# A fused attention and mixture-of-experts kernel: its attention steps issued in another order

## The chip, the cores and the metric

The kernel runs on one NeuronCore of a Trainium2 chip. Time is device time of one execution in microseconds (us); lower is better. The core has four compute engines, each with its own instruction queue that is worked off in order: TensorE (PE in the profile; its weight loads are PEld), VectorE (DVE), ScalarE (ACT) and GpSimd (POOL). SyncE (SP) issues nearly all DMA transfers, in order too. Engines wait for each other through semaphores. TensorE writes its results to PSUM, in banks of 512 f32 per partition; everything else lies in SBUF, 128 partitions wide.

## The reference

Attention over 4 batches, 8 heads, 768 positions of 64 numbers, with a window of 96 positions back, 8 global keys and a bias by distance; then a soft mixture of 8 experts with 4 slots each:

```python
scores = scale * np.matmul(q, k.transpose(0, 1, 3, 2)) + bias   # bias = -slope * distance
scores = np.where(is_global | is_local, scores, -1e9)
a = np.exp(scores - np.max(scores, axis=-1, keepdims=True))
a = a / (np.sum(a, axis=-1, keepdims=True) + 1e-09)
attn = np.matmul(a, v)                       # x: 3072 tokens x 512
...
logits = x @ phi                             # 3072 x 32 slots
d = softmax(logits, over tokens);  slot_input = d.T @ x
h = np.maximum(slot_input[e] @ w1[e], 0);  slot_out[e] = h @ w2[e]   # for each expert e
return softmax(logits, over slots) @ slot_out
```

## The kernel before

Attention is worked off in 16 pairs u of two heads (i = 0, 1), four pairs to a batch. Positions are cut into 7 tiles of 120, and each key tile meets 216 queries; a pair's scores are computed in three steps k = 0, 1, 2 (two, two and three key tiles; the last has 12 matmuls, the others 8). The work is written as steps, small functions that issue a few instructions on one engine. The steps and their engines:

- SyncE: load_qk(u) (832 KB into one of two buffers raw0, raw1), load_v(u), and the experts' weights: 32 pieces of 1 MB. `piece(k)` loads one of the first ten into a buffer of its own; `extra` loads into holes of attention's buffers; `free(i)` loads into a part of an attention buffer once attention is done with it (raw, tb, ph, v16, vt, tt, xta, xtt, xn). A load waits in the queue until what it overwrites has been read, and all loads behind it wait as well.
- TensorE: scores(u,k) (line 522) into one of two PSUM tiles sc0, sc1 by turns; max_t(u), max_b(u) (a transpose and a broadcast of the pair's maximum, lines 538 and 544); values(u,i) (39 matmuls with 39 weight loads, line 579) into x; tr(u,k) (transposes of the result, line 616, four tiles and three); logits(u) for two pairs at a time (line 646); once per batch by_token (line 702) and dispatch (28 matmuls, line 725). `warm` issues matmuls whose result nobody reads.
- VectorE: biased(u,k) (scores plus bias table, with a running maximum, line 531); max_r(u) (line 541); v_lo(u) (line 500, what of V the f16 copy loses); ev_sums, ev_recs, ev_mul(u,i) (division by the sum, lines 592 to 604); the tables; logits_all, strip_max, strip_sum, dispatch_sum once per batch; and tr_copy_dve and w_lo_dve, copies of steps that are else on other engines.
- ScalarE: max_c(u) (line 548), exponential(u,i) (line 552), w_hi(u,i) (the cast to f16, line 555), v_hi_act(u) (line 496), tr_copy (line 621), by_token_copy, lnat_copy, strip_exp.
- GpSimd: w_lo(u,i,part) (what the cast lost, in three parts, line 562), and v_hi for some pairs (line 493).

A pair therefore goes scores, biased, max_t, max_r, max_b, max_c, exponential, w_hi, w_lo, values, ev_mul, tr, tr_copy, logits. The buffers for the cast weights are single for each i (ph0, ph1), so w_hi(u+1,i) waits for values(u,i). The maxima, the transposes, the logits and the dispatch share two PSUM banks (m) by turns. Several pairs are under way at once.

What stands where in each engine's queue is set by one list, ORDER (line 51): 632 entries such as `('scores', 3, 1)`, issued from front to back:

```python
for name, u, *args in ORDER:
    steps[name](u, *args)
```

Each engine gets its own steps in the order of the list; how entries for different engines stand to each other also sets which write counts as earlier, and so some waits. The order of the `free` entries also sets which attention buffer takes which weight piece (`held`). Behind the list come the last batch's softmax and dispatch (last_dispatch), then hidden for two groups of four experts, project, and combine with the output.

Of the kernel before, what the change touches and what calls it, by code (L numbers as in the profile page):

```python
# [1121 lines left out]
```

## Time and profile before

| | us |
|---|---|
| median of 3 runs | 211.16 (210.53 to 211.30) |
| the profiled execution, first to last instruction (span) | 208.9 |
| TensorE busy | 180.1 (86% of the span) |
| VectorE busy | 145.4 (70%) |
| ScalarE busy | 129.5 (62%) |
| GpSimd busy | 105.2 (50%) |
| mean granted TensorE clock | 0.968 of full speed |
| read from HBM, written | 54.59 MB, 6.29 MB |

The profile is of one more execution; for it only the span is known, and it stands 2.3 below the median of the timed runs, which also count what lies around the first and the last instruction. Lines of the profile name an engine, a line of the code, an operation, and out<-in by tile names. In a timeline a row is start, duration, engine, line, operation, tiles, shapes and count; in brackets stands the idle time of the engine just before it and what ended it. Attention's last step, the second half of logits(15), ends near 147 us; the experts' layers fill the rest.

### The profile page before, as it was taken

What the parts mean: (1) busy time and instruction counts of PE and PEld (TensorE: products, weight loads), DVE (VectorE), ACT (ScalarE), POOL (GpSimd) and SP (SyncE); (2) the same over time, 40 slices, a digit from 0 to 9 for tenths busy, and PEclk for the clock granted to TensorE, in tenths of its full rate; (3) what the DMA queues carried; (4) which work ended last, traced back from release to release, by engine and by line L of the source; (5) the groups of instructions that cost most, each with busy time, mean ns of one, the idle gap of its engine ahead of it and who ended that gap; (6) DMA issues with size and microseconds to landing.
All of it is one profiled execution on the core that took longest, in us unless ns stands there. A gap on an engine that the chain in (4) does not pass through costs nothing. (4 is left out here: it accounts for less than half of the span.)

```text
span 208.9 us, 6433 instructions
## 1 busy us (share of the span) xinstructions
PE 180.1 (86%) x2645; PEld 131.2 (63%) x2645; DVE 145.4 (70%) x358; ACT 129.5 (62%) x177; POOL 105.2 (50%) x130
## 2 busy tenths in 40 slices
...
GB/s 109 424 351 393 362 402 397 318 404 416 413 410 370 283 125 135 212 42 254 166 89 244 81 340 354 349 419 367 375 109 326 407 403 387 286 162 344 283 339 108
DMA packets 20631, 61.40 MB, mean 294 GB/s; under 512 B 1904, under 2 KB 9328, under 8 KB 18928
## 3 DMA queue, kind: packets, MB, share of 16 engines
...
q8 instruction: 23, 0.38, 0.7%
...
q10 hardware_dynamic: 144, 0.00, 0.0%
HBM read 54.59 MB, written 6.29 MB: 291 GB/s over the span
## 5 line engine op out<-in xcount | busy, mean ns | idle before, releaser
L562 POOL TENSOR_TENSOR ph<-tb,ph 128x432 f16<-128x432 f32 x92 | 96.6, 1081 | 33.1 <-ACT ph L555 27.7
L522 PE MATMUL sc<-raw 64*128 64x216 f32 (+2 forms) x448 | 48.3, 343 | 3.9 <-DVE mx L531 3.4
L555 ACT CAST ph<-tb 128x1296 f16<-128x1296 f32 x32 | 40.7, 1271 | 9.5 <-PE x L579 8.4
L579 PE MATMUL x<-v,ph 128*128 128x65 f16 (+1 forms) x1248 | 43.6, 194 | 2.7 <-DVE xmax L604 2.2
L579 PEld LDWEIGHTS <-ph 128*128 128x128 f16 x1248 | 40.9, 98 | 7.0 <-issue 5.6
L552 ACT ACTIVATE tb<-tb,nb 128x1296 f32<-128x1296 f32 x32 | 44.0, 1378 | 0.4
L522 PEld LDWEIGHTS sc<-raw 64*128 64x128 f32 x448 | 36.6, 186 | 10.0 <-DVE mx L531 5.0
L604 DVE CUSTOM_DVE_ANT_1 xn<-x,rc 120x448 f32<-120x448 f32 x32 | 19.2, 622 | 4.0 <-PE x L579 3.4
L500 DVE SCALAR_TENSOR_TENSOR v<-vt,v 128x896 f16<-128x896 f32 x16 | 19.8, 1238 | 1.1 <-ACT v L496 1.0
L531 DVE CUSTOM_DVE_ANT_1 tb<-sc,tt,mx 128x864 f32<-128x864 f32 x16 | 17.8, 1113 | 0.9 <-DVE mx L531 0.2
L616 PE MATMUL m<-ident,xn 120*128 120x120 f32 x105 | 14.8, 273 | 2.4 <-DVE xmax L604 1.0
L496 ACT ACTIVATE v<-vt 128x896 f16<-128x896 f32 x12 | 11.3, 944 | 7.4 <-DMA vt<-in_v_dram 7.4
L616 PEld LDWEIGHTS m<-ident,xn 120*128 120x128 f32 x105 | 10.7, 141 | 5.0 <-issue 1.7
L136 PE MATMUL x<-wp,tb 128*32 128x256 f32 x112 | 10.9, 381 | 1.1 <-DVE flag L862 1.1
L106 PE MATMUL hp<-wp,sl 128*32 128x512 f32 x80 | 10.5, 593 | 0.0
L531 DVE CUSTOM_DVE_ANT_1 tb<-sc,xta,mx 128x864 f32<-128x864 f32 x8 | 8.9, 1116 | 1.3 <-PE sc L522 0.8
L531 DVE CUSTOM_DVE_ANT_1 tb<-sc,tt 128x864 f32<-128x864 f32 x8 | 8.5, 1056 | 1.3 <-PE sc L522 0.7
L531 DVE CUSTOM_DVE_ANT_1 tb<-sc,xtt,mx 128x864 f32<-128x864 f32 x8 | 8.9, 1112 | 0.2
L199 ACT COPY ph<-cp 128x512 f32<-128x512 f32 x4 | 2.1, 590 | 10.9 <-PE cp L196 10.9
L136 PEld LDWEIGHTS x<-wp,tb 128*32 128x32 f32 x112 | 5.5, 110 | 3.8 <-DVE flag L862 1.2
L181 DVE TENSOR_SCALAR ohs<-x,sgn 128x256 fp32r<-128x256 f32 x2 | 1.0, 484 | 9.4 <-PE ft L861 4.9
L548 ACT COPY nb<-m 128x1 f32<-128x1 f32 x16 | 2.5, 157 | 7.7 <-PE m L544 7.6
...
## 6 DMA issues: line engine op xcount, KB each, us to landing
raw<-in_qk_dram SPq DMA_DIRECT2D x15, 832.0 KB, 6.3
...
```

The source lines that it names most:

```text
L106: nc.tensor.matmul(out=hp[n][32 * s:32 * s + 32, :], lhsT=slv(a, c, s), rhs=w1(e, c // 2)[:, (c % 2) * DF + 512 * n:(c % 2) * DF + 512 * n ...
L136: nc.tensor.matmul(out=o[32 * s:32 * s + 32, 0:w], lhsT=ht[:, c, 32 * s:32 * s + 32], rhs=w2(4 * a + s, half)[:, c0 + c * w:c0 + c * w + w ...
L496: nc.scalar.activation(out=vhi[u % 2][:, :, :, 0:D], in_=vraw[u % 2], func=AF.Copy, scale=V_SC)
L500: nc.vector.scalar_tensor_tensor(out=vlo[k].rearrange("p j i d -> p (j i) d"), in0=vraw[k].rearrange("p j i d -> p (j i) d"), scalar=V_SC, ...
L522: nc.tensor.matmul(out=z[:, i, at:at + n], lhsT=r_[r, KCOL[j]:KCOL[j] + KR], rhs=r_[r, KW + KB * j:KW + KB * j + n], start=True, stop=True)
L531: nc.vector.tensor_tensor_reduce(out=tb(u)[:, :, BW * k:BW * k + BW], in0=sc[(3 * u + k) % 2][:, :, 0:BW], in1=table.unit(u % NP, k), scal ...
L552: nc.scalar.activation(out=t, in_=t, func=AF.Exp, bias=nbs[u], scale=T_SC)
L555: nc.scalar.copy(out=blocks(phi_[i])[:, :, 0:QW], in_=tb(u)[:, i].rearrange("p (s c) -> p s c", c=QW))
L562: (engine or nc.gpsimd).tensor_tensor(out=blocks(plo_[i])[:, c, 0:QW], in0=tb(u)[:, i].rearrange("p (s c) -> p s c", c=QW)[:, c], in1=bloc ...
L579: nc.tensor.matmul(out=x[:, (D + 1) * t:(D + 1) * t + d], lhsT=w[:, c:c + P], rhs=vv[:, j, i, 0:d], start=(z == 0), stop=(z == len(ops) - ...
L604: nc.vector.tensor_tensor_reduce(out=xnb[(u // 2) % 3][:, :, c:c + D], in0=xv[:, i, :, 0:D], in1=rcs.pop((u, i)).unsqueeze(2).to_broadcast ...
L616: nc.tensor.transpose(out=m[:, at:at + KB], in_=xnb[(u // 2) % 3][:, t, P * (p % 2):P * (p % 2) + P], identity=ident[0:KB, 0:KB])
```

## The change

Only ORDER changes: the same 632 entries in another order. It has no effect on what is computed. The first entries of the list, before and after:

```diff
-ORDER = [('load_qk0', 0), ('load_qk', 0), ('load_v', 0), ('load_qk', 1), ('keys', 0), ('load_v', 1), ('scores', 0, 0), ...
+ORDER = [('keys', 0), ('load_qk0', 0), ('warm', 0, 7), ('table_even', 0), ('table_odd', 0), ('scores', 0, 0), ...
```

Over the whole list, scores steps that follow each other directly on TensorE go from 8 to 13, tr steps from 11 to 4, values steps from 4 to 1. On SyncE the first three pairs' loads of Q and K go ahead of the first piece, phi is loaded later, pieces 3 to 8 are spread over the time up to pair 13, and piece 9 stands at the very end, behind all `free` entries. The three places that matter most:

At the start, on TensorE, from scores(1,0) (raw_94 is pair 1's buffer) to the warm matmuls (L511). Before:

```order
L522 MATMUL sc_173<-raw_94 128x216 x4
L538 MATMUL m<-ident,mx 1x128
L522 MATMUL sc_172<-raw_94 128x216 x4
L544 MATMUL m<-mm_161,bsel 128x1
L511 LDWEIGHTS const-bfloat16-1.0
```

and after:

```order
L522 MATMUL sc_173<-raw_94 128x216 x4
L538 MATMUL m<-ident,mx 1x128
L544 MATMUL m<-mm_161,bsel 128x1
L522 MATMUL sc_172<-raw_94 128x216 x4
L522 MATMUL sc_173<-raw_94 128x216 x2
L522 MATMUL sc_173<-raw_94 128x168 x2
L522 MATMUL sc_173<-raw_94 128x48 x2
L511 LDWEIGHTS const-bfloat16-1.0
```

The maximum of pair 0 (L544) moved ahead of scores(1,1), and scores(1,2) ahead of the ten warm matmuls. A little later max_b(1) moves ahead of values(0,0) in the same way, and on VectorE v_lo(0) and v_lo(1) move from ahead of pair 1's biased steps to between them.

At the third dispatch, on TensorE, behind values(13,1): tr(12,1) and tr(12,0) (L616), the dispatch (L725), max_t(15) (L538) and max_b(15) (L544). Before:

```order
L616 MATMUL m_2255<-ident_78,xn01_106 128x120 x3
L725 MATMUL m_2265<-xn01_106,dn_2259 32x256 x4
L725 MATMUL m_2265<-xn2_105,dn_2259 32x256 x4
L725 MATMUL m_2265<-xn01_106,dn_2259 32x256 x3
L725 MATMUL m_2265<-xn2_105,dn_2259 32x256 x3
L538 MATMUL m_2290<-ident_78,mx_2115 1x128
L616 MATMUL m_2295<-ident_78,xn01_106 128x120 x4
L544 MATMUL m_2290<-mm1_162,bsel_160 128x1
```

and after, where max_t(15) stands ahead of values(13,1) already:

```order
L616 MATMUL m_2260<-ident_78,xn01_106 128x120 x3
L544 MATMUL m_2211<-mm1_162,bsel_160 128x1
L725 MATMUL m_2276<-xn01_106,dn_2208 32x256 x4
L725 MATMUL m_2276<-xn2_105,dn_2208 32x256 x4
L725 MATMUL m_2276<-xn01_106,dn_2208 32x256 x3
L725 MATMUL m_2276<-xn2_105,dn_2208 32x256 x3
```

The last pair's maximum moved ahead of the dispatch; tr(12,0) moved behind values(14,1), where it stands with tr(13,1) and tr(13,0) ahead of values(15,0).

In the same place on ScalarE, from the second exponential of pair 14 (nb_2161, nb_2151) to the second cast of pair 15 (ph1_99). Before:

```order
L552 ACTIVATE tb2_97<-tb2_97,nb_2161 128x1296
L555 CAST ph1_99<-tb2_97 128x6x216
L496 ACTIVATE v16_100<-vt_101 128x14x64
L548 COPY nb_2343<-m_2290 128x1
L621 COPY xta_103<-m_2295 128x480
L552 ACTIVATE tb0_95<-tb0_95,nb_2343 128x1296
L555 CAST ph0_98<-tb0_95 128x6x216
L621 COPY xtt_104<-m_2349 128x480
L552 ACTIVATE tb0_95<-tb0_95,nb_2343 128x1296
L555 CAST ph1_99<-tb0_95 128x6x216
```

and after:

```order
L552 ACTIVATE tb2_97<-tb2_97,nb_2151 128x1296
L621 COPY xta_103<-m_2260 128x288
L548 COPY nb_2271<-m_2211 128x1
L555 CAST ph1_99<-tb2_97 128x6x216
L552 ACTIVATE tb0_95<-tb0_95,nb_2271 128x1296
L496 ACTIVATE v16_100<-vt_101 128x14x64
L555 CAST ph0_98<-tb0_95 128x6x216
L552 ACTIVATE tb0_95<-tb0_95,nb_2271 128x1296
L621 COPY xta_103<-m_2377 128x480
L555 CAST ph1_99<-tb0_95 128x6x216
```

max_c(15) (L548) moved ahead of the second cast of pair 14, and pair 15's first exponential ahead of v_hi_act(15).

2 lines of the change are left out of this document (1 added, 1 removed).

## Prediction

> **What bounds the kernel now.** I read the page for the span and the costliest groups, then busy time by stage, then TensorE's waits, then the timelines of the stages that wait. On the page, the span, two groups (their mean duration stands behind the comma) and one line of the DMA issues (the last number is the median time to landing):
>
> ```profile
> span 208.9 us, 6433 instructions
> ...
> L562 POOL TENSOR_TENSOR ph<-tb,ph 128x432 f16<-128x432 f32 x92 | 96.6, 1081 | 33.1 <-ACT ph L555 27.7
> ...
> L552 ACT ACTIVATE tb<-tb,nb 128x1296 f32<-128x1296 f32 x32 | 44.0, 1378 | 0.4
> ...
> raw<-in_qk_dram SPq DMA_DIRECT2D x15, 832.0 KB, 6.3
> ```
>
> Busy time by stage: start, the even middle, the close of attention, and all that follows it. Behind the length stand PE, PEld, DVE, ACT and POOL with their counts, then TensorE's clock, the DMA share and GB/s:
>
> ```profile
> 0.00:26.00 26.00, 20.70 (x167) 12.14 (x168) 19.87 (x48) 11.76 (x13) 11.43 (x41) 1.00 0.87 328
> 26.00:117.00 91.00, 88.48 (x1524) 73.70 (x1524) 77.94 (x187) 80.22 (x102) 76.83 (x75) 1.00 0.72 269
> 117.00:147.00 30.00, 24.74 (x426) 18.68 (x423) 18.83 (x48) 20.79 (x32) 16.94 (x15) 0.94 0.95 338
> 147.00:209.00 62.00, 46.15 (x536) 26.69 (x536) 28.80 (x76) 16.77 (x33) 0.00 (x0) 0.92 0.81 293
> ```
>
> TensorE idles 2.5 us in the 91 of the middle: there it is the bound. It idles 5.3 us in the 26 of the start and 5.3 in the 30 of the close, where the clock is also below 1. The last 62 us hold none of the reordered steps. Its waits by releaser (total, times, longest):
>
> ```profile
> PE sc L522 <- DVE mx L531: 3.4, 5, 1.3
> PE x L579 <- DVE xmax L604: 2.2, 2, 1.8
> ...
> PE m L702 <- ACT ex L686: 0.9, 1, 0.9
> ```
>
> So a new order can win in the start and in the close, where waits are; in the middle it can win only by making TensorE's own work shorter.
>
> **Nothing is added or removed.** The two tables hold the same 632 steps, so the terms are waits, changes between kinds of work on TensorE, and what the clock does.
>
> **Start.** Rows of the timelines (start, duration, and in brackets the idle time before, with its releaser):
>
> ```profile
> 13.05 1.09 DVE L500 SCALAR_TENSOR_TENSOR v<-vt,v 128x896 f16<-128x896 f32 x1
> ...
> 16.40 1.06 DVE L531 CUSTOM_DVE_ANT_1 tb<-sc,tt 128x864 f32<-128x864 f32 x1
> ```
>
> ```profile
> 22.45 0.38 PE L544 MATMUL m<-mm,bsel 2*128 2x1 f32 x2
> ...
> 25.04 1.00 PE L522 MATMUL sc<-raw 64*128 64x216 f32 x8 [1.21 <-DVE mx L531]
> 25.98 1.36 PE L579 MATMUL x<-v,ph 128*128 128x65 f16 x39
> ```
>
> ```profile
> 22.87 0.16 ACT L548 COPY nb<-m 128x1 f32<-128x1 f32 x1 [2.60 <-PE m L544]
> ```
>
> ```profile
> 25.87 5.84 POOL L562 TENSOR_TENSOR ph<-tb,ph 128x432 f16<-128x432 f32 x6 [1.90 <-ACT ph L555]
> ```
>
> ```profile
> 18.63 0.33 SPq L389 DMA_DIRECT2D raw<-in_qk_dram  x1
> ```
>
> These are v_lo(0); the first bias of pair 1; max_b(1), scores(3,0), values(0,1); max_c(1); the first low parts of pair 1; and load_qk(3). Before, VectorE runs v_lo(0), max_r(0), two tables and v_lo(1) ahead of pair 1's first bias at 16.40. Now only one table and max_r(0) stand ahead, the bias comes at about 14.0, and both v_lo are spread between the biases. The maximum of pair 1 is no longer behind values(0,0) on TensorE (a values step is about 1.3 us): max_c(1) goes from 22.87 to about 21.1, and its exponentials with it, so GpSimd's 1.90 us idle ahead of pair 1 nearly closes. scores(3,0) is put down to VectorE, whose bias had left that bank at 22.4; what came at 25 was load_qk(3), issued 18.63 plus the median 6.3. Now scores(1,2) stands ahead of the ten warm matmuls, load_qk(3) leaves some 2.4 us sooner, and fewer weight pieces share the DMA. Against it: v_hi_act(1), 0.94, now stands between pair 0's first exponential and its cast, where the exponential is only 0.5 us sooner, so pair 0's low parts end 0.3 later than before's 23.97 (25.87 less 1.90). values(0,1) then comes at 24.4 instead of 25.98. I take **-1.5**; the ends are -1.9 (all of GpSimd's idle time) and +0.4 (only the v_hi_act remains, if the load lands no earlier). The warm matmuls put ahead of scores(0,0) cost nothing: the first bias waits for the tables until 9.5, and two score steps take 2 us from 6.9.
>
> **Middle.** TensorE's rows; a step's cost is the distance to the next start:
>
> ```profile
> 45.10 0.91 PE L616 MATMUL m<-ident,xn 120*128 120x120 f32 x7
> 45.94 1.87 PE L522 MATMUL sc<-raw 64*128 64x216 f32 x20
> ...
> 49.30 1.00 PE L522 MATMUL sc<-raw 64*128 64x216 f32 x8
> 50.23 0.38 PE L544 MATMUL m<-mm,bsel 2*128 2x1 f32 x2
> ...
> 56.19 1.73 PE L522 MATMUL sc<-raw 64*128 64x216 f32 x16
> 57.85 0.38 PE L544 MATMUL m<-mm,bsel 2*128 2x1 f32 x2
> ...
> 69.66 0.63 PE L616 MATMUL m<-ident,xn 120*128 120x120 f32 x4
> 70.22 1.00 PE L522 MATMUL sc<-raw 64*128 64x216 f32 x8
> ...
> 73.79 0.53 PE L616 MATMUL m<-ident,xn 120*128 120x120 f32 x3
> 74.25 1.07 PE L522 MATMUL sc<-raw 64*128 64x216 f32 x12
> ```
>
> One score step costs 0.93 (49.30 to 50.23), two together 1.66 (56.19 to 57.85): 0.20 saved per adjacency. But the two transposes of a pair cost 0.84 together (45.10 to 45.94) and 0.56 + 0.46 = 1.02 apart: 0.18 lost. Counted on the table between pair 2's and pair 15's scores, score steps that follow each other go from 5 to 9, transposes that do from 9 to 1. That is 8 x 0.18 = +1.4, 4 x 0.20 = -0.8 (less where a k=2 step with more matmuls is one of the two), and two adjacent values steps lost, put at 0.1 each, +0.2: some +0.8 to +1.2. I take **+1.2**, the upper end, since most new adjacencies have a k=2 step. The waits of the middle I leave at 2.5 us: some of the old go, some new come. Ends: -1.3 (all old waits gone) and +5 (0.3 us more per pair).
>
> **Close.** Rows of TensorE, ScalarE and VectorE, and TensorE's clock by stretch:
>
> ```profile
> 124.90 2.52 PE L579 MATMUL x<-v,ph 128*128 128x65 f16 x78 [0.42 <-DVE xmax L604]
> ...
> 137.19 2.12 PE L579 MATMUL x<-v,ph 128*128 128x65 f16 x39 [1.77 <-DVE xmax L604]
> ...
> 141.42 1.35 PE L579 MATMUL x<-v,ph 128*128 128x65 f16 x39
> ...
> 146.10 0.89 PE L646 MATMUL sc<-xta,phis 128*32 128x240 f32 x8 [0.65 <-ACT xta L621]
> ```
>
> ```profile
> 126.32 1.27 ACT L555 CAST ph<-tb 128x1296 f16<-128x1296 f32 x1 [0.65 <-PE x L579]
> ...
> 131.68 0.16 ACT L548 COPY nb<-m 128x1 f32<-128x1 f32 x1
> ...
> 136.74 1.27 ACT L555 CAST ph<-tb 128x1296 f16<-128x1296 f32 x1
> ```
>
> ```profile
> 138.04 1.94 DVE L562 TENSOR_TENSOR ph<-tb,ph 128x432 f16<-128x432 f32 x2 [0.90 <-ACT ph L555]
> ```
>
> ```profile
> 136.00:140.00 4.00, 2.81 (x49) 2.51 (x51) 3.08 (x6) 2.23 (x3) 2.82 (x3) 0.68 1.03 431
> 140.00:144.00 4.00, 4.00 (x63) 2.41 (x57) 1.13 (x5) 1.50 (x4) 0.00 (x0) 0.89 0.99 384
> ```
>
> values(13,0) at 124.90 stands behind by_token(11), which waited 0.9 for ScalarE, and waits 0.42 more for ev_mul(12,1). Now scores(15,2) and max_b(14) fill the first wait, and ev_mul(12,0) runs ahead of the logits' sum: **-1.3**. Then pair 15. Its max_c was at 131.68, because max_t(15) stood behind the whole third dispatch; so its second cast came at 136.74, and values(15,1) ended at 142.8. Now max_c(15) comes right behind the second exponential of pair 14, both exponentials of pair 15 are done when values(14,1) ends, and from there to the end of values(15,1) lie: tr(12,0) 0.56, its copy 0.55, the cast 1.27, VectorE's two low parts 1.94, and the last third of values 0.6: 4.9 us. Before, values(14,1) ended at 135.4 (137.19 less 1.77), and it took 7.3. That is **-2.4**. The dispatch pays for it: its PSUM bank is that of max_t(15), so it now waits for max_c(15) behind an exponential, some 0.7 us; that lies in the wait of values(14,1) for the low parts. tr(13,0) waits for the copy of tr(12,0), inside the same 4.9. In the 7.3 lies a half clock: 0.32 and 0.11 of two 4 us stretches, doubled, are 3.4 us at half speed, which starts behind the wait of 1.77; it made values(15,0) 2.12 instead of 1.35, and 3.4 us at half speed with TensorE nearly always busy are some 1.5 lost. With three transposes between values(14,1) and values(15,0) that wait breaks into pieces under 1 us.
>
> [...]
>
> **Queues.** SyncE's queue changes most: pair loads go ahead, weight pieces 3 to 9 later, piece 9 to the very end, behind xta's part, which only logits2(15) frees:
>
> ```profile
> 147.08 0.33 SPq L372 DMA_DIRECT2D xta<-in_w_dram  x1
> ```
>
> At about 143 there will follow 0.4 + 1.0 + 1.0 MB, 6.5 us at the close's 338 to 431 GB/s, so piece 9 lands near 151. The hidden layer needs it at its second half, some 9 us after logits2 plus 7 for the first half: 158 or so. Covered by 6 us; if the queue is later than that, the loss is the difference. On GpSimd the low parts change places within a pair, at no cost: values needs all of them.
>
> **Sum.** -1.5 + 1.2 - 1.3 - 2.4 = -4.0. The span goes from 208.9 to 204.9. The median of the runs, 211.16, lies 2.3 over the span; I keep that: **207.2 us**.
>
> **Rivals.** (1) *The half clock comes again in the close*: nothing excludes it, since several waits remain there; +1.5: 208.7. (2) *Piece 9 comes late*: the DMA is at 0.95 in the close already; it needs over 6 us of further backlog; with 2.5 us of loss beyond that 209.7. (3) *The middle eats it*: new waits of 0.33 us per pair over 12 pairs are 4.0: 211.2. (4) *Slower*: the loop through one weight buffer is values 1.3, cast 1.27, three low parts 3 x 1.08, 5.8 us, in a pair's 7.6 (91 us for 12). TensorE runs in order, so where a scores step or a split transpose stands ahead of values whose parts are ready, the loop and ScalarE's queue get later and the next pair too. From 0.42 us per pair it decides for slower; at 0.6 it is 7.2: 214.4. For it speaks that GpSimd waits 27.7 us for the casts, so this loop is already felt; against it that TensorE waits only 2.5 us in the middle and the other three engines have 10 us or more of idle time there.
>
> **Chances.** Forecast 0.48, between 205.2 and 209.2 by the ends of start and close; (1) 0.12; (2) 0.06; (3) 0.14; (4) 0.20. A measurement of this kernel tells 0.5%, 1.06 us. Faster: 0.48 + 0.12 + 0.05 = 0.65; same: 0.01 + 0.14 = 0.15; slower 0.20. The range 204.0 to 213.0 leaves out a twentieth below (the old waits of the middle gone too) and the worse half of (4).
>
> **What would show it.** values(0,1) near 24.4. Between 26 and 117 PE busy near 90 and idle near 2.5; if idle is 6 or more, (3) or (4). max_c(15) some 4 us sooner against values(13,0); no wait over 1.2 us of PE behind it; clock 1.00 in the close; logits2(15) ending near 143. First matmul of the hidden layer's second half without a wait for DMA. Most likely to make me wrong: waits of the middle, which the trace of before can't show.

## The result, and the profile after

Four executions of the changed kernel took 201.23, 201.38, 203.21 and 203.44 us, median 202.30; before, beside them, 210.84. The ratio is 0.9611 (95% interval 0.9549 to 0.9673): faster by 8.5 us, twice the 4.0 forecast, and below the range given for the time. The sign was right. The profiled execution took 201.23, with a span of 199.4 instead of 208.9.

The page of the profile after, the lines that answer to those shown of before:

```profile
span 199.4 us, 6439 instructions
...
L562 POOL TENSOR_TENSOR ph<-tb,ph 128x432 f16<-128x432 f32 x92 | 96.5, 1079 | 25.1 <-ACT ph L555 23.4
```

Busy time by stretch (PE, PEld, DVE, ACT, POOL, then TensorE's clock, DMA share, GB/s):

```profile
0.00:26.00 26.00, 22.97 (x210) 14.18 (x212) 21.27 (x53) 13.04 (x14) 13.29 (x42) 1.00 0.76 281
26.00:117.00 91.00, 89.49 (x1560) 75.88 (x1558) 81.71 (x199) 82.22 (x105) 79.56 (x77) 1.00 0.83 299
117.00:147.00 30.00, 26.15 (x425) 18.38 (x428) 21.12 (x64) 17.72 (x32) 12.24 (x12) 1.00 0.94 357
```

TensorE's waits (total, times, longest). The first answers to 3.4 us in before; the 2.2 us that values waited in before for VectorE's division are gone:

```profile
PE sc L522 <- DVE mx L531: 1.2, 2, 1.0
...
PE sc L522 <- DMA raw<-in_qk_dram: 0.9, 1, 0.9
...
PE m L616 <- ACT xta L621: 0.6, 1, 0.6
PE m L725 <- ACT nb L548: 0.6, 1, 0.6
```

The timelines at the places of the prediction (start, duration, operation, idle time before): load_qk(3), the low parts of pairs 0 and 1, max_c(1), values(0,1); scores(15,0), values(13,0), the third dispatch, the transposes behind values(14,1), values(15,1), the end of logits2(15) and the hidden layer's second half; max_c(15) and the last cast; piece 9.

```profile
15.93 0.33 SPq L389 DMA_DIRECT2D raw<-in_qk_dram  x1
```

```profile
17.84 12.37 POOL L562 TENSOR_TENSOR ph<-tb,ph 128x432 f16<-128x432 f32 x12 [11.52 <-ACT ph L555]
```

```profile
20.56 0.16 ACT L548 COPY nb<-m 128x1 f32<-128x1 f32 x1 [0.22 <-PE m L544]
```

```profile
23.96 1.54 PE L579 MATMUL x<-v,ph 128*128 128x65 f16 x39
...
112.16 1.00 PE L522 MATMUL sc<-raw 64*128 64x216 f32 x8
...
118.52 1.34 PE L579 MATMUL x<-v,ph 128*128 128x65 f16 x39
...
122.83 1.93 PE L725 MATMUL m<-xn,dn 120*32 120x256 f32 x28 [0.57 <-ACT nb L548]
...
127.68 0.91 PE L616 MATMUL m<-ident,xn 120*128 120x120 f32 x7
129.17 0.63 PE L616 MATMUL m<-ident,xn 120*128 120x120 f32 x4 [0.57 <-ACT xta L621]
...
131.62 1.47 PE L579 MATMUL x<-v,ph 128*128 128x65 f16 x39
...
136.48 0.90 PE L646 MATMUL sc<-xta,phis 128*32 128x240 f32 x8 [0.17 <-ACT xta L621]
...
151.30 0.60 PE L106 MATMUL hp<-raw,sl 128*32 128x512 f32 x2
```

```profile
122.68 0.16 ACT L548 COPY nb<-m 128x1 f32<-128x1 f32 x1
...
129.02 1.27 ACT L555 CAST ph<-tb 128x1296 f16<-128x1296 f32 x1
```

```profile
138.32 0.60 SPq L372 DMA_DIRECT2D wp<-in_w_dram  x1
```

GpSimd's 1.90 us idle between pairs 0 and 1 is gone: its first twelve low parts run without a gap. By stage, between the same steps of both profiled executions:

| us | before | after | difference | forecast |
|---|---|---|---|---|
| start: to values(0,1) | 25.98 | 23.96 | -2.0 | -1.5 |
| middle: to scores(15,0) | 91.3 | 88.2 | -3.1 | +1.2 |
| close: to the end of logits2(15) | 29.7 | 25.2 | -4.5 | -3.7 |

The span got 9.5 shorter. The median got about one less shorter, because in half of its executions the changed kernel has a loss that the profiled one has not (see e12_after_again).

Where the middle's 3.1 came from shows when the distance from each TensorE step to the next, less the idle time, is added up by kind, over all steps of the middle (scores(15,0) of before starts 0.93 ahead of the values at 118.20, by the price of a lone score step; the forecast's terms add up to +0.8, of which it took the upper end, +1.2):

| us | before | after | difference | forecast |
|---|---|---|---|---|
| scores | 33.5 | 32.5 | -1.0 | -0.8 |
| transposes of the result (tr) | 10.3 | 9.9 | -0.4 | +1.4 |
| values | 29.9 | 29.6 | -0.3 | +0.2 |
| max_t, max_b | 5.9 | 5.4 | -0.5 | 0 |
| idle | 2.2 | 1.3 | -0.9 | 0 |

Of the 0.4 at tr, 0.36 is tr(10,1), which now stands behind scores(15,0), so that work went from the middle to the close.

### The profile page after: what moved, and what is told of

It is laid out like the page before. It is cut to its first block, busy times and chain, and to the rows that moved or that the text cites. A ratio compares the mean times of both kernels' runs of the same rounds, so it can differ in the third digit from the quotient of the medians.

```text
span 199.4 us, 6439 instructions
## 1 busy us (share of the span) xinstructions
PE 176.5 (88%) x2645; PEld 130.7 (66%) x2645; DVE 145.9 (73%) x358; ACT 128.2 (64%) x177; POOL 105.1 (53%) x130
## 5 line engine op out<-in xcount | busy, mean ns | idle before, releaser
L562 POOL TENSOR_TENSOR ph<-tb,ph 128x432 f16<-128x432 f32 x92 | 96.5, 1079 | 25.1 <-ACT ph L555 23.4
L522 PE MATMUL sc<-raw 64*128 64x216 f32 (+2 forms) x448 | 46.5, 340 | 2.1 <-DVE mx L531 1.2
L500 DVE SCALAR_TENSOR_TENSOR v<-vt,v 128x896 f16<-128x896 f32 x16 | 21.3, 1328 | 0.5 <-ACT v L496 0.5
L616 PE MATMUL m<-ident,xn 120*128 120x120 f32 x105 | 16.3, 275 | 1.0 <-ACT xta L621 0.6
L616 PEld LDWEIGHTS m<-ident,xn 120*128 120x128 f32 x105 | 10.9, 140 | 3.4 <-issue 1.7
L136 PE MATMUL x<-wp,vt 128*32 128x256 f32 x112 | 10.9, 381 | 1.1 <-DVE flag L862 1.1
L106 PE MATMUL hp<-wp,sl 128*32 128x512 f32 x80 | 10.5, 593 | 0.0
L136 PEld LDWEIGHTS x<-wp,vt 128*32 128x32 f32 x112 | 5.5, 110 | 3.8 <-DVE flag L862 1.2
L106 PEld LDWEIGHTS hp<-wp,sl 128*32 128x32 f32 x80 | 2.9, 110 | 6.6 <-issue 6.3
```

Of the source, the lines that this page charges most:

```text
L106: nc.tensor.matmul(out=hp[n][32 * s:32 * s + 32, :], lhsT=slv(a, c, s), rhs=w1(e, c // 2)[:, (c % 2) * DF + 512 * n:(c % 2) * DF + 512 * n ...
L136: nc.tensor.matmul(out=o[32 * s:32 * s + 32, 0:w], lhsT=ht[:, c, 32 * s:32 * s + 32], rhs=w2(4 * a + s, half)[:, c0 + c * w:c0 + c * w + w ...
L500: nc.vector.scalar_tensor_tensor(out=vlo[k].rearrange("p j i d -> p (j i) d"), in0=vraw[k].rearrange("p j i d -> p (j i) d"), scalar=V_SC, ...
L522: nc.tensor.matmul(out=z[:, i, at:at + n], lhsT=r_[r, KCOL[j]:KCOL[j] + KR], rhs=r_[r, KW + KB * j:KW + KB * j + n], start=True, stop=True)
L562: (engine or nc.gpsimd).tensor_tensor(out=blocks(plo_[i])[:, c, 0:QW], in0=tb(u)[:, i].rearrange("p (s c) -> p s c", c=QW)[:, c], in1=bloc ...
L616: nc.tensor.transpose(out=m[:, at:at + KB], in_=xnb[(u // 2) % 3][:, t, P * (p % 2):P * (p % 2) + P], identity=ident[0:KB, 0:KB])
```

## The experiments

Twelve runs follow, in four groups; a group shares its runs of before (medians 211.20, 211.23, 210.95, 209.91). The ratios are to these.

**Stages alone.** The list of one kernel up to a step, the rest in the order of the other.

```diff
# e1_start: after up to ('values', 0, 1), then before
# e2_close: before up to ('scores', 15, 0), then after
# e3_start_middle: after up to ('scores', 15, 0), then before
```

> The order of after up to values(0,1), all that follows in the order of before. Theory (the three stages add up, each carries its own gain): values(0,1) near 24.0 instead of 25.98, and the 2.0 us stay to the end, because TensorE idles only 2.5 us in the middle: about 208.8. Rival (the middle's waits are behind other engines, so an earlier start is given back there): 210 to 211, with scores(15,0) as late as in before.

Measured: 212.97 to 215.26 in three executions and 217.08 in a fourth, ratio 1.0165 (1.0054 to 1.0276). Both theories missed; it is slower. Its timeline of TensorE at pair 4:

```profile
30.19 1.34 PE L579 MATMUL x<-v,ph 128*128 128x65 f16 x39
34.59 1.42 PE L522 MATMUL sc<-raw 64*128 64x216 f32 x8 [3.06 <-DMA raw<-in_qk_dram]
```

Phi, an extra and piece 2 stand ahead of load_qk(4) here, which after has behind it; piece 1 stands ahead of it in both (the wait in after is 0.86). Behind that wait the clock is halved for 3.4 us from 35.0 on (0.70 is the mean of this stretch, the number behind ACT's and POOL's), and in the first 26 us its mean is 0.87.

```profile
36.00:40.00 4.00, 4.00 (x55) 3.45 (x56) 2.49 (x8) 1.49 (x3) 0.33 (x1) 0.70 1.04 412
```

> The order of before up to scores(15,0), all that follows in the order of after. Theory (the stages add up): start and middle as before, from scores(15,0) to the end of logits2(15) 25.2 instead of 29.8 us, clock 1.00 in the close: about 206.3. Rival (the close gains only because the other engines arrive there further ahead): under 2.5 us gained, over 208.3. The prediction's price of the close, 3.7, would give 207.1.

Measured: 207.43 (206.13 to 208.26), ratio 0.9861 (0.9788 to 0.9933). In its profiled execution (206.13) the close is 24.9 long with clock 1.00, 25.2 in after less the 0.36 of tr(10,1) that before's middle holds; start and middle are before's. So the close gains by itself; the median is 1.1 over the theory, since two executions, at 208.09 and 208.26, have a lower clock over the span (0.967 and 0.970 instead of 0.976 and 0.977), and no trace shows where.

> The order of after up to scores(15,0), the close in the order of before. Theory (the middle gains 3.0 us by itself, 2.0 the start): scores(15,0) near 112.2 as in after, the close again 29.8 long with its wait of 1.8 and the half clock: about 205.8. By the prediction's terms (start -1.5, middle +1.2) it would be 210.5.

Measured: 205.99, ratio 0.9794 (0.9691 to 0.9897). The close took 29.5, as expected. But values(0,1) came at 26.3, not 24.0, with clock 0.87 in the first 26 us, and the middle took 87.4, 0.8 less than in after. That the median lies near 205.8 all the same is luck in part: the start is 2.3 longer than expected, and the middle and the close are shorter.

**The price of a split.**

```diff
# e4_joined, after with, for pairs 0-4 and 6-8, for example:
-('tr', 2, 1), ..., ('values', 3, 1), ..., ('max_t', 5), ..., ('tr', 2, 0), ..., ('tr_copy', 2, 0)
+('tr', 2, 1), ('tr', 2, 0), ..., ('tr_copy', 2, 1), ('tr_copy', 2, 0), ..., ('values', 3, 1), ..., ('max_t', 5)
```

> After, with the two transposes of pairs 0, 1, 2, 3, 4, 6, 7 and 8 next to each other again (the later half and its copy moved to the earlier one). By the prediction's price of a split, 0.18 each, this gains 1.4 us: scores(15,0) near 110.7, about 200.9. Theory (a step's cost depends on what follows it, and a half ahead of values costs 0.36 or 0.44, together no more than the seven at once): TensorE's work in the middle within 0.3 of after's, scores(15,0) near 112.2 or later by what the earlier copies push back on ScalarE, 202 to 203.

Measured: 204.17 (202.66 to 204.50), ratio 0.9669 (0.9595 to 0.9743): no gain, a loss. Its middle took 88.7; that of after took 87.2 in the profiled execution that has the same clock of 0.87 in the start (e12_after_again). The tr steps together cost 9.81 against 9.95 there, 0.14 saved where 1.44 was forecast; waits and the steps around them took more than that. The rows of after show why: a half ahead of a values step costs 0.46 and 0.34 (start to next start), 0.80 together, and the seven at once cost 0.74 ahead of values (e4_joined, last fence). The prediction had priced the halves by rows ahead of score steps, at 0.56 and 0.46:

```profile
34.50 0.63 PE L616 MATMUL m<-ident,xn 120*128 120x120 f32 x4
34.96 1.34 PE L579 MATMUL x<-v,ph 128*128 128x65 f16 x39
...
39.07 0.27 PE L538 MATMUL m<-ident,mx 128*1 128x128 f32 x1
39.18 0.47 PE L616 MATMUL m<-ident,xn 120*128 120x120 f32 x3
...
44.68 0.50 PE L616 MATMUL m<-ident,xn 120*128 120x120 f32 x3
45.02 1.35 PE L579 MATMUL x<-v,ph 128*128 128x65 f16 x39
```

```profile
39.57 0.91 PE L616 MATMUL m<-ident,xn 120*128 120x120 f32 x7 [0.48 <-DVE xmax L604]
40.31 1.35 PE L579 MATMUL x<-v,ph 128*128 128x65 f16 x39
```

The same holds for max_t: 0.11 ahead of another transpose or of values (39.07 to 39.18), 0.20 ahead of scores; before, 8 of the middle's 12 stood ahead of scores, now 3. Transposes stand ahead of a score step 8 times before and 9 times after.

**The start.**

```diff
# e5_no_start: before up to ('values', 0, 1), then after
# e6_warm: after with
-('warm', 0, 7), ('table_even', 0), ('table_odd', 0), ('scores', 0, 0), ('biased', 0, 0), ('load_qk', 0), ('scores', 0, 1),
+('table_even', 0), ('table_odd', 0), ('scores', 0, 0), ('biased', 0, 0), ('load_qk', 0), ('scores', 0, 1), ('warm', 0, 7),
# e7_start_queue: e1_start, with that edit, and phi and pieces 1 to 8 behind load_qk(4) to load_qk(14)
# e11_warm3: e6_warm with
-('warm', 0, 7)
+('warm', 0, 3)
# e12_after_again: after
```

> The order of before up to values(0,1) (the seven warm matmuls behind scores(0,1) again), all that follows in the order of after. Theory (after's start is worth 2.0 us in the executions whose clock stays whole there, nothing in the others, and the rest gains 7.5 by itself): values(0,1) at 26.0, middle 87.4 to 88.2, close 25.2, clock 1.00 up to 26 us: about 203, and no execution above 204. Rival (the middle needs after's start): 205 or more.

Measured: 202.56 to 202.97 in four executions, 204.42 in the profiled one, which has a half clock at 26.0 behind a wait of 1.9 for load_qk(3); median 202.81, ratio 0.9616 (0.9570 to 0.9662). As the theory has it but for that one. Against e6_warm, which differs from it in the start, it is 1.7 slower: that much of the start's 2.0 stays to the end.

> After, with one entry moved: the seven warm matmuls behind scores(0,1), as in before, instead of ahead of scores(0,0). Theory (the half clock in the start comes because TensorE waits 1.0 to 1.8 us for the tables straight behind scores(0,1), and the warm matmuls had filled that): clock 1.00 up to 26 us in every execution, all of them near 201.3, none near 203.4. Rival (the half clock hangs on the short waits at max_t(0) and max_b(0), or on when the first loads arrive): half of the executions stay near 203.4. By the prediction's words, moving these matmuls costs nothing: no change.

Measured: 200.96 to 202.13 in six executions, median 201.15, ratio 0.9555 (0.9517 to 0.9592), clock 0.973 to 0.978 over the whole span in all.

> The changed kernel as it is, six more executions, against e6_warm's six (201.0 to 202.1, clock 0.973 to 0.978). Theory (without the seven warm matmuls behind scores(0,1) the half clock of the start comes in a good part of the executions): some of the six near 203.3 with a clock near 0.962, the others near 201.3 with 0.978, nothing between. Rival (the two values of after were chance, the same would come with e6_warm): all near 201.3, or both kernels alike.

Measured: 202.47, ratio 0.9618 (0.9562 to 0.9674): three executions at 202.71 to 203.47 with clock 0.956 to 0.961, three at 200.93 to 202.22 with 0.976 to 0.979. With the first four that is five of ten with the lower clock, against none of six of e6_warm, and none of the ten of e8_scores_apart and e10_close2, which have e6_warm's start. Its profiled execution is one of them; first 26 us, and the first score steps:

```profile
0.00:26.00 26.00, 23.00 (x164) 14.16 (x166) 19.70 (x47) 11.14 (x12) 11.76 (x40) 0.87 0.70 265
```

```profile
7.32 1.73 PE L522 MATMUL sc<-raw 64*128 64x216 f32 x16
10.64 1.07 PE L522 MATMUL sc<-raw 64*128 64x216 f32 x12 [1.59 <-DVE mx L531]
11.92 1.40 PE L522 MATMUL sc<-raw 64*128 64x216 f32 x8 [0.20 <-DVE mx L531]
```

0.13 of 26 us, doubled, are 6.8 us at half clock, from 12.4 to 19.2; values(0,1) comes at 26.4 instead of 23.96. e6_warm, same stretch:

```profile
0.00:26.00 26.00, 22.35 (x208) 13.71 (x210) 20.92 (x51) 12.83 (x14) 13.06 (x42) 1.00 0.75 280
```

> As e1_start (start of after, the rest of before), but with the seven warm matmuls behind scores(0,1), and with phi and the weight pieces 1 to 8 behind the pair loads on SyncE's queue as in after. Theory (e1_start lost its gain to pieces that stood ahead of load_qk(4), a wait of 3.1 us with a half clock behind it, and to the half clock of the start): values(0,1) at 24.0, no DMA wait over 1 us, scores(15,0) near 115.5: 208.5 to 209.3. Rival (the middle of before can't use an earlier start): 210.5 or more.

Measured: 207.82, ratio 0.9864 (0.9824 to 0.9903); values(0,1) at 24.2, scores(15,0) at 115.7, no DMA wait among TensorE's longest. It is 0.7 under the theory. In its profiled execution the close, in the order of before, took 28.2 with a clock of 1.00, where before took 29.7 with a half clock; two of eight executions, at 209.3, have 0.966 and 0.967 over the span instead of 0.973 to 0.977. So the middle of before can use the earlier start, if phi and the weight pieces stay behind the pair loads.

> As e6_warm, with three of the seven warm matmuls behind scores(0,1) left out (their result is read by nobody). TensorE then waits about 2.0 us for the tables, and in the 3.4 us up to 12.0 it works some 1.3 us instead of 2.0. Theory (what counts is the share of work in 3.4 us, and half of it or less can halve the clock: the half clocks so far began behind 0.4 to 1.7 us of work, no stretch of over 1.8 had one): the half clock of the start comes back in some or all executions, with 203 there. [...]

Three of the seven stay and four are left out (the text above has it the other way round). Measured: median 202.95: 203.34, 203.48 and 202.57 with clock 0.961 to 0.962, 201.02 with 0.978. The profiled execution (203.34):

```profile
10.64 1.08 PE L522 MATMUL sc<-raw 64*128 64x216 f32 x12 [2.15 <-DVE mx L531]
11.92 1.63 PE L522 MATMUL sc<-raw 64*128 64x216 f32 x8 [0.20 <-DVE mx L531]
```

```profile
0.00:26.00 26.00, 22.22 (x158) 13.62 (x160) 19.96 (x47) 11.15 (x12) 11.75 (x40) 0.87 0.70 265
```

With a gap of 2.15 us instead of the 1.03 of e6_warm the half clock is back in three of four.

**Score steps.**

```diff
# e8_scores_apart: e6_warm with, for example (also pairs 4, 11 and 12):
-('scores', 3, 1), ..., ('scores', 3, 2), ('max_b', 2),
+('scores', 3, 1), ..., ('max_b', 2), ('scores', 3, 2),
```

> As e6_warm, with four of the score steps that follow each other taken apart again (max_b of pairs 2, 4, 11 and 12 put between them, as in before). Theory (an adjacency is worth 0.20, less where a k=2 step is one of the two): TensorE's work in the middle 0.5 to 0.8 longer, about 202. Rival (the earlier max_b lets ScalarE start sooner and pays for it): the time of e6_warm or less.

Measured: 201.68, ratio 0.9568 (0.9523 to 0.9613), not told apart from e6_warm's 0.9555. In the middle, scores cost 33.2 instead of 32.25: 0.24 for each adjacency, and TensorE idled 0.4 instead of 1.0. Both were right in part: the adjacency is worth its price, and the waits that come with the later max_b give about two thirds of it back.

**The close.**

```diff
# e9_max_late: e6_warm with
-('max_t', 15), ..., ('max_r', 15), ('values', 13, 1), ..., ('max_b', 15), ..., ('max_c', 15), ..., ('exponential', 15, 0), ..., ('dispatch', 11),
+('values', 13, 1), ..., ('dispatch', 11), ('dispatch_sum', 11), ('max_t', 15), ('max_r', 15), ('tr', 12, 0), ('max_b', 15), ('max_c', 15), ('tr_copy', 12, 0), ('exponential', 15, 0),
# e10_close2: e6_warm with, among others,
-('v_hi_act', 15)
+('v_hi', 15)
-('w_lo', 14, 0, 0)
+('w_lo_dve', 14, 0, 0)
```

> As e6_warm, with the last pair's maximum back behind the third dispatch as in before: max_t(15), max_r(15), tr(12,0), max_b(15) and max_c(15) behind dispatch(11) and its sum, the first exponential of pair 15 behind them. Theory (half of the close's gain is this move, priced at 2.4 in the prediction): max_c(15) 4 to 5 us later against values(13,0), from the end of values(14,1) to the end of values(15,1) 7 us instead of 5.4, a wait of over 1.2 us on TensorE there, perhaps with a half clock behind it: 202.8 to 204.5. Rival (the early max_c only hands the wait to the dispatch, which waits 0.57 for it, and to the transposes): 201.2 to 202.

Measured: 203.46 (203.04 to 203.81), ratio 0.9666 (0.9606 to 0.9726): 2.3 over e6_warm. max_c(15), and TensorE ahead of values(15,0):

```profile
124.76 0.16 ACT L548 COPY nb<-m 128x1 f32<-128x1 f32 x1 [1.50 <-PE m L544]
```

```profile
127.03 0.91 PE L616 MATMUL m<-ident,xn 120*128 120x120 f32 x7
130.25 0.49 PE L579 MATMUL x<-v,ph 128*128 128x65 f16 x11 [2.30 <-DVE xmax L604]
131.22 1.71 PE L579 MATMUL x<-v,ph 128*128 128x65 f16 x28 [0.48 <-DVE ph L562]
```

max_c(15) comes 6.9 us behind the start of values(13,0), 4.2 in e6_warm; that is 2.8 later, not 4 to 5, but the rest holds: from the end of values(14,1) to that of values(15,1) it takes 8.0 instead of 5.2 in e6_warm, with a wait of 2.30 and a half clock behind it (130.97 to 134.38), and by their clocks (0.968 to 0.969) in all four executions.

> As e6_warm, with the waits that are left in the close taken on: v_hi(15) on GpSimd instead of ScalarE, one low part of pair 14 on VectorE instead, v_lo(15) ahead of the dispatch's sum, both exponentials of pair 15 ahead of its casts, max_c(15) ahead of the copy of tr(12,1), load_v(15) right behind v_lo(13), and piece 2 behind load_qk(6). Theory (ScalarE, busy without a gap from 119.9 to 130.6, sets the close): dispatch's wait 0.57 down to 0.3, second cast of pair 15 some 0.6 sooner, load wait at pair 4 gone: 200.0 to 200.6. Rival (GpSimd and VectorE are as full there, and slow each other): 201 or more.

Measured: 202.56, ratio 0.9624 (0.9574 to 0.9674): 1.4 worse than e6_warm, as the rival has it. GpSimd, VectorE and TensorE around values(14,1):

```profile
123.77 1.39 POOL L493 TENSOR_SCALAR v<-vt 128x896 f16<-128x896 f32 x1
125.13 5.71 POOL L562 TENSOR_TENSOR ph<-tb,ph 128x432 f16<-128x432 f32 x5
```

```profile
125.19 1.89 DVE L500 SCALAR_TENSOR_TENSOR v<-vt,v 128x896 f16<-128x896 f32 x1 [0.84 <-POOL v L493]
```

```profile
128.00 0.81 PE L579 MATMUL x<-v,ph 128*128 128x65 f16 x21 [1.61 <-POOL ph L562]
```

v_hi took 1.39 on GpSimd (0.93 to 0.95 at every other place in the traces), ahead of the low parts that values(14,1) waits for. v_lo(15) took 1.89 beside GpSimd's work, but it took 1.93 in e6_warm as well, so that is no part of the loss. What the run was to mend did get shorter in the close (dispatch's wait 0.33, that of tr(13,0) 0.34), but a wait of 1.61 came in: the close took 26.3 instead of 25.2. The middle took 88.5 instead of 87.6, with a wait of 1.15 for the load at pair 4, which was to be gone. e6_warm stays the best of all.

## Why the prediction was off

**Start, -1.5: right in size, with a hole.** max_c(1) came at 20.56 (forecast 21.1), values(0,1) at 23.96 (24.4), load_qk(3) 2.7 us sooner, all by the steps named. But "The warm matmuls put ahead of scores(0,0) cost nothing" failed. Behind scores(0,1) they had filled a wait that no row called expensive. Without them TensorE works as little as 1.6 us in the 3.4 up to 12.4 us, and 6.8 us at half clock follow, which take the start's gain (values(0,1) at 26.4, in the profiled execution of e12_after_again); five of ten executions have its low clock over the span (0.956 to 0.963). The rival of a half clock was there, but only for the close.

**Middle, +1.2: the step that failed.** The span's gain was missed by 5.5 us (9.5 against 4.0), and 4.3 of them lie here. The 8 x 0.18 = +1.4 for the splits was priced by rows in which both halves stand ahead of a score step. What makes a half dear there is the way into a score step, some 0.1 us (0.56 and 0.46 there, 0.46 and 0.34 ahead of values), and a split adds no such way: transposes stand ahead of a score step 9 times after and 8 before, and the other halves stand ahead of values, logits and maxima. There two halves cost 0.80 against 0.74, and joining eight pairs again saved 0.14 (e4_joined). In place of +1.4 stands -0.4, of which 0.36 is the moved tr(10,1). The adjacencies were priced right (0.20; 0.24 in e8_scores_apart), but they also leave four ways into a score step fewer, and max_t, which stands ahead of one 3 times instead of 8, got cheaper where the prediction had 0. The waits, which I had left alone, fell by 0.9. That max_t and values got cheaper by what follows them, and why the waits fell, is read from the traces, not tested alone; e8_scores_apart shows only that max_b's place is one of the causes of waits.

**Close, -3.7, found -4.5.** The waits ahead of values(13,0) gave 1.3, as forecast. From the end of values(14,1) to that of values(15,1) it is 5.2 (forecast 4.9), 2.1 instead of 2.4 won, since tr(13,0) waits 0.57 for the copy of tr(12,0); max_c(15) came 2.6 us sooner against values(13,0), not some 4. The 1.5 that the prediction put down to the half clock is borne out by e7_start_queue, whose close in the order of before took 28.2 without one. The 1.2 that the prediction did not have lies between values(13,0) and the end of values(14,1), 10.5 before and 9.3 now: tr(12,0) and both transposes of pair 13, 1.3 us of TensorE's work, moved from there into the wait behind it. e9_max_late puts the move of the maximum back, with tr(12,0) and the half clock that follows, at 2.3.

**Queues, 0: right.** Piece 9 is issued at 138.3; the hidden layer's second half began at 151.3 without a wait for DMA. But e1_start shows that this freedom is not general: with phi, an extra and piece 2 ahead of load_qk(4) TensorE waits 3.06 us for it, and e7_start_queue, which has them behind it, has no such wait.

**The rivals.** The half clock in the close did not come (1.00 in the profiled execution). Between scores(15,0) and the end of logits2(15) no 3.4 us hold less than 2.4 us of TensorE's work, where before had 1.3; the half clocks of all runs began behind 1.7 or less (last section). Slower, through the loop over the cast weights, did not happen: GpSimd's wait for the casts fell from 27.7 to 23.4.
